# Row sums of four heads in one transfer on ScalarE's queue, decay rows of a pair in one load from DRAM, normalise steps two to a slot, and constants moved off VectorE, in a kernel of forgetting attention followed by a gated feed-forward block

## The chip, the cores and the metric

The kernel runs on one core of a Trainium2 chip. The metric is the device time of one execution, in microseconds (us). Each version was run several times, in alternation with the kernel before on the same chip, and the medians are quoted. The span of a profiled execution is some 2 us shorter than its time; where stages are compared, spans are used.

## The reference

For 8 batches of 8 heads (64 heads in all), 576 positions and a head dimension of 64, causal attention is computed with a decay: `cum` is the running sum of `log(clip(f))`, and `cum[i] - cum[j]` is added to the scaled score of positions i and j. The heads are put side by side and go through a gated feed-forward block (FFN).

```python
scores = scale * np.matmul(q, k.transpose(0, 1, 3, 2))
cum = np.cumsum(np.log(np.clip(f, 0.0001, 1.0)), axis=-1)
scores = scores + cum[:, :, :, None] - cum[:, :, None, :]     # where not causal: -1e9
attn = softmax(scores)                                        # row sums + 1e-9
x = (attn @ v).transpose(0, 2, 1, 3).reshape(4608, 512)
g = x @ w_gate                                                # 512 -> 1536
out = (g * sigmoid(g) * (x @ w_val)) @ w_out                  # 1536 -> 512
```

## The kernel before

The kernel works in slots, a quarter of a head each. A table `todo` says what is issued in which slot; instructions keep that order on each engine. Heads come in pairs, and pairs in groups of four heads. The decay is added by TensorE: q and k get four more rows, so that the scores matmul contracts 68 rows. The value matmul has columns of ones next to v, so it also yields the row sums of exp.

From slot 47 on, the FFN of the first eight heads runs between the attention of the next eight, on the same engines. The parts that the change touches:

```python
    def rows(p):                       # decay rows of a pair: four small transfers
        b = p % NBUF
        hs = slice(2 * p, 2 * p + 2)
        nc.sync.dma_start(out=QT[b][D : D + 1], in_=cq[hs])
        for r in range(3):
            nc.sync.dma_start(out=KT[b][D + 1 + r : D + 2 + r, :, :S], in_=ck[hs, r])

    def collect(h):                    # row sums of one head, spread over 32 partitions
        g, j = h // GH, h % GH
        ...
        nc.sync.dma_start(out=SC[g][j * n : (j + 1) * n, :], in_=E[h][row : row + 1, :])

    def recip(g):                      # one reciprocal for four heads, then to DRAM
        rc = rp.tile([P, GH * S // P], F32, name="rc", tag="rc")
        nc.vector.reciprocal(rc, SC.pop(g))
        nc.sync.dma_start(out=rc_dram[g].rearrange("(p c) -> p c", p=P), in_=rc)

    def spread(g):                     # broadcast of the reciprocals, in two halves
        ...
            nc.sync.dma_start(
                out=rb[a * D : (a + 1) * D],
                in_=src[a].unsqueeze(0).to_broadcast([D, GH // 2, S]),
            )
    ...
        at(s0 - 14, rows, p)
    ...
        at(s0 + 4 + LAG, collect, h)
        if h % GH == GH - 1:
            g = h // GH
            at(s0 + 6 + LAG, recip, g)
            at(s0 + 8 + LAG, spread, g)
            for j in range(GH):
                at(s0 + 12 + LAG + j, normalise, g * GH + j)      # one to a slot
```

`normalise` multiplies a head's values by its reciprocals on VectorE and writes `xT`, which FFN reads. All loads of q, k and v go through SyncE's queue; the FFN weights go through GpSimd's, in ten chunks.

The softmax here doesn't subtract the row's maximum and nothing guards it: scores larger than these inputs give would overflow.

Of the kernel before, what the change touches and what calls it, by code (L numbers as in the profile page):

```python
# [11 lines left out]
ALU = mybir.AluOpType  # L12
# [12 lines left out]
NSLOT = len(BANKS)  # L25
LAG = 3


@with_exitstack
def kernel(ctx, tc, q, k, v, f, w_gate, w_val, w_out, out):  # L30
# [22 lines left out]
    ptp = ctx.enter_context(tc.tile_pool(name="ptp", bufs=3))  # L53
    evp = ctx.enter_context(tc.tile_pool(name="evp", bufs=8))
    rp = ctx.enter_context(tc.tile_pool(name="rp", bufs=2))
    ps_ffn = ctx.enter_context(tc.tile_pool(name="ps_ffn", bufs=4, space=PSUM))
    ps_s = ctx.enter_context(tc.tile_pool(name="ps_s", bufs=2, space=PSUM))
    ps_t = ctx.enter_context(tc.tile_pool(name="ps_t", bufs=1, space=PSUM))
    ps_o = ctx.enter_context(tc.tile_pool(name="ps_o", bufs=1, space=PSUM))
    rc_dram = nc.dram_tensor("rc_d", (BH // GH, GH * S), F32, kind="Internal").ap()  # L60
    order = ctx.enter_context(tc.manual_schedule())

    NBUF = 3
    QT = [consts.tile([KR, 2, S], BF16, name=f"QT{i}") for i in range(NBUF)]
    KT = [consts.tile([KR, 2, NB * P], BF16, name=f"KT{i}") for i in range(NBUF)]
    VB = [consts.tile([P, NB, 2, P], BF16, name=f"VB{i}") for i in range(NBUF)]
    cq = consts.tile([BH, S], BF16, name="cq")
    ck = consts.tile([BH, 3, S], BF16, name="ck")
    wg = wpool.tile([P, KD, DFF], BF16, name="wg")
# [22 lines left out]
    def rows(p):  # L92
        b = p % NBUF
        hs = slice(2 * p, 2 * p + 2)
        nc.sync.dma_start(out=QT[b][D : D + 1], in_=cq[hs])
        for r in range(3):
            nc.sync.dma_start(out=KT[b][D + 1 + r : D + 2 + r, :, :S], in_=ck[hs, r])

    def cast(p, nm):
        if nm == "v":  # L100
            b = p % NBUF
            vn = nat.pop(("v", p))
            for j in range(2):
                nc.gpsimd.tensor_copy(VB[b][:, : NB - 1, j, j * D : j * D + D], vn[:, : NB - 1, j])
                nc.gpsimd.tensor_copy(VB[b][:LAST, NB - 1, j, j * D : j * D + D], vn[:LAST, NB - 1, j])
            return
        t = bfp.tile([P, NB, 2 * D], BF16, name=f"b_{nm}", tag=f"b_{nm}")
        src = nat.pop((nm, p)).rearrange("p n h d -> p n (h d)")
        nc.gpsimd.tensor_copy(t[:, : NB - 1], src[:, : NB - 1])  # L109
        nc.gpsimd.tensor_copy(t[:LAST, NB - 1], src[:LAST, NB - 1])  # L110
        nat["b" + nm, p] = t

    def transposes(p, nm):
        dst = (QT if nm == "q" else KT)[p % NBUF]
        src = nat.pop(("b" + nm, p))
        t = ps_t.tile([P, S], BF16, name="tp", tag="t")
        for n in range(NB):
            w = P if n < NB - 1 else LAST
            nc.tensor.transpose(t[:, n * P : n * P + w], src[:w, n, :], ident[:w, :w])  # L119
        for a in range(2):  # L120
            nc.vector.tensor_copy(dst[:D, a, :S], t[a * D : (a + 1) * D])  # L121

    PT, O, E = {}, {}, {}

    def qk(h, i):
# [6 lines left out]
        for kt, q0, w in BANKS[i]:  # L132
            nc.tensor.matmul(  # L133
                s[:, c : c + w], KT[b][:, j, kt * P : (kt + 1) * P], QT[b][:, j, q0 : q0 + w],
                start=True, stop=True,
            )
            c += w
        off = OFFS[i]
        nc.scalar.activation(pt[:, off : off + c], s[:, :c], AF.Exp, scale=0.125)  # L139
        c = off  # L140
        for kt, q0, w in BANKS[i]:
            if q0 <= kt * P:
                m = min(P, w)
                nc.gpsimd.affine_select(  # L144
                    out=pt[:, c : c + m], in_=pt[:, c : c + m],
                    pattern=[[1, m]], compare_op=ALU.is_ge, fill=0.0, base=0, channel_multiplier=-1,
                )
            c += w

    def pv(h, i):  # L150
# [15 lines left out]
        if last:  # L166
            if half == 0:
                E[h] = evp.tile([P, S], F32, name="ev", tag="ev")
            dst = E[h][:, q_lo : q_lo + q_n]
            if h < H:  # L170
                nc.vector.tensor_copy(dst, o[:, :q_n])
            else:
                nc.scalar.activation(dst, o[:, :q_n], AF.Copy)
            O.pop((h, half))

    SC, RB = {}, {}

    def collect(h):
        g, j = h // GH, h % GH
        if j == 0:  # L180
            SC[g] = rp.tile([P, GH * S // P], F32, name="sc", tag="sc")
        row = D if j % 2 == 0 else 0
        n = P // GH
        nc.sync.dma_start(out=SC[g][j * n : (j + 1) * n, :], in_=E[h][row : row + 1, :])

    def recip(g):
        rc = rp.tile([P, GH * S // P], F32, name="rc", tag="rc")
        nc.vector.reciprocal(rc, SC.pop(g))  # L188
        nc.sync.dma_start(out=rc_dram[g].rearrange("(p c) -> p c", p=P), in_=rc)

    def spread(g):
        rb = rp.tile([P, GH // 2, S], F32, name="rb", tag="rb")
        src = rc_dram[g].rearrange("(r a s) -> a r s", a=2, s=S)
        for a in range(2):
            nc.sync.dma_start(
                out=rb[a * D : (a + 1) * D],
                in_=src[a].unsqueeze(0).to_broadcast([D, GH // 2, S]),
            )
        RB[g] = rb

    def normalise(hd):
        g, j = hd // GH, hd % GH
        a = j % 2
        b0 = (hd // H) * S
        nc.vector.tensor_mul(  # L205
            xT[a * D : (a + 1) * D, (hd % H) // 2, b0 : b0 + S],
            E.pop(hd)[a * D : (a + 1) * D],
            RB[g][a * D : (a + 1) * D, j // 2],
        )
# [38 lines left out]
    with tc.tile_pool(name="ini", bufs=1) as ini:  # L248
        lf = ini.tile([BH, S], F32, name="lf")
        nc.scalar.dma_start(out=lf, in_=f.rearrange("b h s -> (b h) s"))  # L250
        for part in (0, 1, 2):
            load(0, "q", part)
            load(0, "k", part)
        for part in (0, 1, 2):
            load(0, "v", part)
        ident = consts.tile([P, P], BF16, name="ident")
        make_identity(nc, ident[:, :])
        zero = ini.tile([BH, S], F32, name="zero")
        nc.gpsimd.memset(zero, 0.0)
        for i in range(NBUF):  # L260
            nc.vector.memset(QT[i][D:KR], 1.0)
            nc.vector.memset(KT[i][D:KR], 1.0)
            nc.gpsimd.memset(KT[i][:, :, S:], 0.0)
        nc.vector.tensor_scalar(out=lf, in0=lf, scalar1=1e-4, scalar2=1.0, op0=ALU.max, op1=ALU.min)
        nc.scalar.activation(lf, lf, AF.Ln)
        cum = ini.tile([BH, S], F32, name="cum")
        nc.vector.tensor_tensor_scan(out=cum, data0=lf, data1=zero, initial=0.0, op0=ALU.add, op1=ALU.add)
        nc.scalar.activation(cq, cum, AF.Copy, scale=8.0)
        nc.vector.tensor_scalar_mul(ck[:, 0], cum, -8.0)
        r1 = ini.tile([BH, S], F32, name="r1")  # L270
        nc.vector.scalar_tensor_tensor(out=r1, in0=cum, scalar=-8.0, in1=ck[:, 0], op0=ALU.mult, op1=ALU.subtract)
        nc.vector.tensor_copy(ck[:, 1], r1)
        nc.vector.tensor_sub(ck[:, 2], r1, ck[:, 1])
        for i in range(NBUF):
            nc.vector.memset(VB[i], 1.0)
            nc.vector.memset(VB[i][LAST:, NB - 1], 0.0)
    fp = ctx.enter_context(tc.tile_pool(name="fp", bufs=3))
# [9 lines left out]
    for p in range(NP):  # L287
        s0 = 2 * NSLOT * p
        if p > 0:
            n = 0  # L290
            for nm in ("q", "k", "v"):
                for part in range(3):
                    at(s0 - 24 + n, load, p, nm, part)
                    n += 1
        at(s0 - 14, rows, p)
        at(s0 - 11, cast, p, "q")
# [4 lines left out]
    for h in range(BH):  # L301
# [3 lines left out]
        for i in range(NSLOT):  # L305
            at(s0 + i + LAG, pv, h, i)
        at(s0 + 4 + LAG, collect, h)
        if h % GH == GH - 1:
            g = h // GH
            at(s0 + 6 + LAG, recip, g)  # L310
            at(s0 + 8 + LAG, spread, g)
            for j in range(GH):
                at(s0 + 12 + LAG + j, normalise, g * GH + j)

# [6 lines left out]
    for c in range(4):  # L321
        lo, hi = c * DFF // 4, (c + 1) * DFF // 4
        at(NSLOT * (4 + 2 * c), weights, wg, w_gate, lo, hi, True)
        at(NSLOT * (4 + 2 * c) + 2, weights, wv, w_val, lo, hi, True)
    for c in range(2):
        at(NSLOT * (12 + 2 * c), weights, wo, w_out, c * KF // 2, (c + 1) * KF // 2, False)


    ffn = ffn_stream()
    PER_TILE = 2 * KF * KD + KF * MT // P  # L330
    first = NSLOT * (H - 1) + 12 + LAG + GH
    n_mm = 0
    end = NSLOT * BH + LAG + 12 + GH
    for s in range(min(todo), end):
# [40 lines left out]
```

## Time and profile before

| | before |
|---|---|
| time, median of three runs | 486.08 us (485.72 to 486.36) |
| span of the profiled run | 486.3 us |
| TensorE busy | 86% |
| first scores matmul | 21.5 us |
| first gate matmul (FFN begins) | 96.6 us |
| first output matmul of token tile 0 | 132.6 us |
| the same of tile 5 (attention still running) | 366.1 us |

How to read such a profile: the share of a whole span averages over stages that have different limits. The slices show where the stages lie. Within a stage, the waits say which engine stood for what, and the engine's order in time says why the thing it stood for was late. The prediction quotes the lines of this profile.

### The profile page before, as it was taken

How to read it: one execution, taken by the hardware profiler on the slowest of the kernel's cores; microseconds unless marked ns; L12 is line 12 of the kernel's file. 1: busy time of each engine (PE TensorE's matmuls, PEld its weight loads, DVE VectorE, ACT ScalarE, POOL GpSimd, SP SyncE). 2: the span in 40 equal slices, each digit the busy share in tenths (PEclk: the TensorE clock that was granted, in tenths of full speed). 3: DMA queues.
4: the chain of work that ended last, by engine and by line, in shares of the span. 5: the costliest groups of instructions: out<-in, count | busy, mean ns of one | idle time of the engine just before them, and what ended most of it. 6: DMA issues, size and time to landing. Idle time of an engine off the chain costs nothing.

```text
span 486.3 us, 7925 instructions
## 1 busy us (share of the span) xinstructions
PE 420.5 (86%) x2470; PEld 228.3 (47%) x2512; DVE 280.1 (58%) x458; ACT 241.5 (50%) x516; POOL 201.1 (41%) x596
## 2 busy tenths in 40 slices
PE   0295374398899999999999999999899999999996
PEld 0163242254455555555555555555455554444442
DVE  7742250445936784586468556936593676473570
ACT  2253133256456666666666556656565664232321
POOL 3275285145355455455545464545454631000000
PEclk9999999999999999999999999999999999999999
DMA  5358499589364536453746464555455120401102
GB/s 107 74 119 144 106 150 189 112 139 168 84 166 120 124 90 161 125 124 89 171 115 134 107 165 108 127 129 143 109 122 135 55 51 1 137 0 44 44 0 88
DMA packets 136794, 53.18 MB, mean 109 GB/s; under 512 B 122096, under 2 KB 127984, under 8 KB 136752
## 3 DMA queue, kind: packets, MB, share of 16 engines
q1 hardware_dynamic: 130880, 47.80, 41.0%
q0 software_dynamic: 5792, 4.72, 7.1%
q8 instruction: 20, 0.33, 0.3%
q14 instruction: 22, 0.18, 0.1%
q10 hardware_dynamic: 80, 0.15, 0.1%
HBM read 47.33 MB, written 9.58 MB: 117 GB/s over the span
## 4 chain that ended last, share of the span: by engine, by line
PE 70%; DMA 13%; DVE 8%; issue 3%; SPq 2%; ACT 2%; POOL 1%; DVEq 0%; ACTq 0%; POOLq 0%
PE fo L238 18%; PE gp L221 16%; PE vp L229 16%; PE s L133 7%; DMA rb<-rc_d 6%; PE tp L119 4%; DMA sc<-ev 3%; DMA nat_q<-in_q_dram 3%; DVE xT L205 2%; DMA rc_d<-rc 1%; DVE th L225 1%; ACT pt L139 1%; POOL pt L144 1%; SPq L82 1%; DMA nat_k<-in_k_dram 0%
## 5 line engine op out<-in xcount | busy, mean ns | idle before, releaser
L139 ACT ACTIVATE pt<-s 128x384 bf16<-128x384 f32 (+2 forms) x256 | 128.3, 503 | 132.2 <-PE s L133 131.3
L144 POOL TENSOR_SCALAR_AFFINE_SELECT pt<-pt 128x128 bf16<-128x128 bf16 (+1 forms) x320 | 99.6, 322 | 188.3 <-ACT pt L139 187.7
L221 PE MATMUL gp<-xT,wg 128*128 128x512 bf16 x412 | 116.1, 380 | 5.9 <-DVE th L225 4.4
L229 PE MATMUL vp<-xT,wv 128*128 128x512 bf16 x422 | 117.8, 379 | 2.1 <-DVE hh L232 1.5
L238 PE MATMUL fo<-wo,hh 128*128 128x512 bf16 x420 | 102.2, 378 | 0.7
L225 DVE SCALAR_TENSOR_TENSOR th<-th,gp 128x512 f32<-128x512 f32 x108 | 74.2, 687 | 48.8 <-ACT th L224 48.0
L224 ACT ACTIVATE th<-gp 128x512 f32<-128x512 f32 x108 | 64.6, 598 | 42.0 <-PE gp L221 40.2
L232 DVE TENSOR_TENSOR hh<-th,vp 128x512 bf16<-128x512 f32 x108 | 74.2, 687 | 10.0 <-PE vp L229 0.6
L205 DVE TENSOR_TENSOR xT<-ev,rb 64x576 bf16<-64x576 f32 x64 | 52.8, 825 | 40.0 <-DMA rb<-rc_d 38.8
L221 PEld LDWEIGHTS <-wg 128*128 128x128 bf16 x432 | 39.8, 97 | 39.8 <-issue 4.7
L238 PEld LDWEIGHTS <-hh 128*128 128x128 bf16 x432 | 39.5, 97 | 38.9
L229 PEld LDWEIGHTS <-wv 128*128 128x128 bf16 x432 | 39.4, 97 | 38.0 <-issue 3.0
L242 ACT ACTIVATE ot<-fo 128x512 f32<-128x512 f32 x36 | 21.5, 597 | 32.4 <-PE fo L238 29.2
L133 PE MATMUL s<-QT_90,KT_93 68*128 68x320 bf16 (+4 forms) x154 | 32.5, 286 | 1.2 <-DVE KT_93 L121 0.5
L188 DVE RECIPROCAL rc<-sc 128x18 f32<-128x18 f32 x16 | 4.2, 265 | 50.4 <-DMA sc<-ev 43.7
L133 PE MATMUL s<-QT_91,KT_94 68*128 68x320 bf16 (+4 forms) x154 | 32.6, 284 | 0.4
L161 PEld LDWEIGHTS <-VB_98 128*128 128x128 bf16 x140 | 12.5, 103 | 39.7 <-issue 14.7
L133 PE MATMUL s<-QT_92,KT_95 68*128 68x320 bf16 (+4 forms) x140 | 29.8, 286 | 0.4
L119 PE MATMUL tp<-ident,b_k 128*128 128x128 bf16 (+1 forms) x160 | 18.4, 232 | 11.8 <-DVE QT_90 L121 9.8
L119 PE MATMUL tp<-ident,b_q 128*128 128x128 bf16 (+1 forms) x160 | 18.4, 232 | 9.7 <-POOL b_q L109 9.7
L119 PEld LDWEIGHTS <-b_k 128*128 128x128 bf16 (+1 forms) x160 | 13.8, 105 | 22.4 <-issue 13.5
L119 PEld LDWEIGHTS <-b_q 128*128 128x128 bf16 (+1 forms) x160 | 13.7, 105 | 21.5 <-POOL b_q L109 9.7
(312 smaller groups left out, 413.3 us busy)
## 6 DMA issues: line engine op xcount, KB each, us to landing
rb<-rc_d SPq DMA_DIRECT2D x32, 288.0 KB
out_dram<-ot SPq DMA_DIRECT2D x36, 256.0 KB
nat_q<-in_q_dram SPq DMA_DIRECT2D x64, 128.0 KB
nat_k<-in_k_dram SPq DMA_DIRECT2D x64, 128.0 KB
nat_v<-in_v_dram SPq DMA_DIRECT2D x64, 128.0 KB
wg<-in_moe_w_gate_dram POOLq DMA_DIRECT2D x4, 384.0 KB, 6.2
wv<-in_moe_w_val_dram POOLq DMA_DIRECT2D x4, 384.0 KB, 7.9
wo<-in_moe_w_out_dram POOLq DMA_DIRECT2D x2, 768.0 KB, 9.1
```

Source lines behind the costliest of these rows:

```text
L119: nc.tensor.transpose(t[:, n * P : n * P + w], src[:w, n, :], ident[:w, :w])
L133: nc.tensor.matmul(s[:, c : c + w], KT[b][:, j, kt * P : (kt + 1) * P], QT[b][:, j, q0 : q0 + w], start=True, stop=True,)
L139: nc.scalar.activation(pt[:, off : off + c], s[:, :c], AF.Exp, scale=0.125)
L144: nc.gpsimd.affine_select(out=pt[:, c : c + m], in_=pt[:, c : c + m], pattern=[[1, m]], compare_op=ALU.is_ge, fill=0.0, base=0, channel_mu ...
L205: nc.vector.tensor_mul(xT[a * D : (a + 1) * D, (hd % H) // 2, b0 : b0 + S], E.pop(hd)[a * D : (a + 1) * D], RB[g][a * D : (a + 1) * D, j / ...
L221: nc.tensor.matmul(g_, wg[:, ko, fs], xT[:, ko, ts], start=(ko == 0), stop=(ko == KD - 1))
L224: nc.scalar.activation(th, g_, AF.Tanh, scale=0.5)
L225: nc.vector.scalar_tensor_tensor(out=th, in0=th, scalar=1.0, in1=g_, op0=ALU.add, op1=ALU.mult)
L229: nc.tensor.matmul(v_, wv[:, ko, fs], xT[:, ko, ts], start=(ko == 0), stop=(ko == KD - 1))
L232: nc.vector.tensor_mul(h_, th, v_)
L238: nc.tensor.matmul(o, hh[fc][:, ms * P : (ms + 1) * P], wo[:, fc, :], start=(fc == 0), stop=(fc == KF - 1))
L242: nc.scalar.activation(ot, o, AF.Copy, scale=0.5)
```

## The change

The intent is to relieve SyncE, which issues nearly all transfers, and VectorE. Four decay-row transfers of a pair become one load from a copy in DRAM; q and k of a pair share a tile `QK` for this. Four row-sum transfers of a group become one, on ScalarE's queue, where the reciprocal's store and the broadcast go too. The normalise steps move later and come two to a slot. Memsets move from VectorE to GpSimd, k of the first two pairs is loaded through ScalarE's queue, and the weights are issued a little earlier. Some parts are not in the cuts below: the v casts of the first six pairs move to VectorE, evictions write 65 rows instead of 128 and stay on VectorE for four heads more. The core of the diff, with cuts:

```diff
+NORM = 18
...
-    evp = ctx.enter_context(tc.tile_pool(name="evp", bufs=8))
+    evp = ctx.enter_context(tc.tile_pool(name="evp", bufs=2))
...
     def rows(p):
-        nc.sync.dma_start(out=QT[b][D : D + 1], in_=cq[hs])
-        for r in range(3):
-            nc.sync.dma_start(out=KT[b][D + 1 + r : D + 2 + r, :, :S], in_=ck[hs, r])
+        nc.sync.dma_start(
+            out=QK[p % NBUF][D:KR, :, :S],
+            in_=dec_dram[2 * p : 2 * p + 2].rearrange("j w r s -> r (j w) s"),
+        )
...
-        nc.sync.dma_start(out=SC[g][j * n : (j + 1) * n, :], in_=E[h][row : row + 1, :])
+        nc.scalar.dma_start(out=SC[g], in_=E[g][D : D + 1].rearrange("p j s -> p (j s)"))
...
-        nc.sync.dma_start(out=rc_dram[g].rearrange("(p c) -> p c", p=P), in_=rc)
+        nc.scalar.dma_start(out=rc_dram[g].rearrange("(p c) -> p c", p=P), in_=rc)
...
+        nc.scalar.dma_start(
+            out=RB[g].rearrange("p j s -> p (j s)"), in_=rc_dram[g].unsqueeze(0).to_broadcast([D, GH * S])
+        )
...
-            nc.vector.memset(QT[i][D:KR], 1.0)
-            nc.vector.memset(KT[i][D:KR], 1.0)
-            nc.gpsimd.memset(KT[i][:, :, S:], 0.0)
+            nc.gpsimd.memset(QK[i][:, 1::2, S:], 0.0)
+            nc.gpsimd.memset(VB[i][:, :, :, D:], 1.0)
...
+        nc.scalar.dma_start(out=dec_dram, in_=dec)
...
-            at(s0 + 6 + LAG, recip, g)
-            at(s0 + 8 + LAG, spread, g)
+            at(s0 + 4 + LAG, collect, g)
+            at(s0 + 10 + LAG, recip, g)
+            at(s0 + 13 + LAG, spread, g)
             for j in range(GH):
-                at(s0 + 12 + LAG + j, normalise, g * GH + j)
+                at(s0 + NORM + LAG + j // 2, normalise, g * GH + j)
...
-        at(NSLOT * (4 + 2 * c), weights, wg, w_gate, lo, hi, True)
+        at(NSLOT * (3 + 2 * c), weights, wg, w_gate, lo, hi, True)
```

## The prediction

> **What bounds the kernel now.** I read the page first, then its slices, the sums by window, the waits, the SyncE queue in order of time, and single groups. TensorE is busy for 86% of 486.3 us, which alone would say "TensorE-bound, nothing to gain"; the slices say where that is untrue.
>
> ```profile
> PE   0295374398899999999999999999899999999996
> ...
> DMA  5358499589364536453746464555455120401102
> ```
>
> Each digit is a slice of 12.2 us. From slice 10 on TensorE is at 8 or 9 tenths; before it, holes. The windows (us; then busy time and count of PE, PEld, DVE, ACT, POOL; clock; DMA share; GB/s) put numbers on it:
>
> ```profile
> 25.00:36.00 11.00, 10.71 (x60) 7.04 (x59) 5.60 (x13) 6.02 (x12) 8.54 (x30) 1.00 0.53 120
> 36.00:57.00 21.00, 7.24 (x39) 4.46 (x38) 3.99 (x10) 4.01 (x8) 6.99 (x21) 1.00 0.68 119
> 57.00:73.00 16.00, 12.67 (x69) 7.95 (x68) 8.51 (x16) 6.79 (x14) 12.51 (x32) 1.00 0.88 155
> 73.00:97.00 24.00, 9.69 (x47) 5.51 (x47) 5.14 (x11) 6.94 (x17) 9.17 (x29) 1.00 0.85 149
> 97.00:125.00 28.00, 24.45 (x147) 13.10 (x148) 16.24 (x28) 15.01 (x33) 12.63 (x38) 1.00 0.79 142
> 125.00:225.00 100.00, 97.71 (x621) 54.38 (x632) 66.94 (x111) 61.58 (x138) 50.94 (x152) 1.00 0.52 126
> ```
>
> So three stages: a start until the first scores matmul at 21.5 us; attention alone until the first gate matmul at 96.6 us, with TensorE idle for about half of it; then attention and FFN together, 98% busy. Only the first two can yield much. What stops the second is in the waits (engine, line, what it waited for; total us, times, longest) and in SyncE's queue (start, duration):
>
> ```profile
> DVE rc L188 <- DMA sc<-ev: 43.7, 12, 14.0
> ...
> PE o_559 L161 <- DVE ev L171: 13.5, 1, 13.5
> ```
>
> ```profile
> 43.77 0.60 SPq L184 DMA_DIRECT2D sc<-ev  x1
> 44.42 0.57 SPq L82 DMA_DIRECT2D nat_k<-in_k_dram  x1
> 45.05 0.63 SPq L87 DMA_DIRECT2D nat_k<-in_k_dram  x1
> 45.80 1.07 SPq L82 DMA_DIRECT2D nat_v<-in_v_dram  x2
> 46.97 0.55 SPq L184 DMA_DIRECT2D sc<-ev  x1
> 47.95 0.66 SPq L87 DMA_DIRECT2D nat_v<-in_v_dram  x1
> 48.73 1.07 SPq L82 DMA_DIRECT2D nat_q<-in_q_dram  x2
> 49.90 0.67 SPq L95 DMA_DIRECT2D QT_91<-cq  x1
> 50.62 1.79 SPq L97 DMA_DIRECT2D KT_94<-ck  x3
> 52.46 0.68 SPq L87 DMA_DIRECT2D nat_q<-in_q_dram  x1
> 53.23 0.54 SPq L82 DMA_DIRECT2D nat_k<-in_k_dram  x1
> ```
>
> The last fence is one pair of heads: nine loads, four decay rows, two row sums, 15 issues from 43.77 to 53.77, with hardly a gap. SyncE needs **10.0 us a pair, 0.67 us an issue**. TensorE, while undisturbed (25 to 36 us), starts a head every 3.62 us (scores of head 2 at 28.67, head 3 at 32.30), 7.24 us a pair. SyncE therefore falls behind; VectorE stands at the reciprocal, in its order, for a row sum that SyncE has not yet issued; evictions and transposed copies lie behind it, and TensorE behind those. The bound of this stage is SyncE's issue time.
>
> **What the Trainium skill says.** (1) "DMA: Bandwidth & Descriptors", section "Issuing engines are not separate DMA queues": transfers of all queues interleave on the same 16 engines, and another issuer saves only the sequencer's time, "usually small relative to the DMA itself". The trace agrees on what would be saved but not that it is small: at 0.54 to 0.68 us an issue it bounds a stage. (2) "Perfetto Trace Analysis", section "DMA Instruction — HWDGE (DVE, Sync)": a profiled issue starts when its semaphores are satisfied and ends before the data have moved. So 0.6 us is sequencer time; the chain shows landings apart (sc 1.89 us, rc_d 1.64, rb 4.29 for the first group). (3) "TensorE: Matmul & The Clock Gate", Part 1: 1.2 GHz cold, 2.4 GHz after some 3.4 us of sustained activity. Both speeds are in the trace: the longest value matmul (320 columns) takes 474 ns before FFN starts and 310 after. But TensorE is 97% busy for 11 us (25 to 36) and stays slow, so I count attention alone at the cold rate whatever the change does.
>
> **The change part by part.** A slot is a quarter of a head: 0.906 us cold.
>
> *Decay rows and row sums leave SyncE.* Four row transfers of a pair become one load; two row sums, and each group's reciprocal and broadcast, go to ScalarE's queue, one transfer each per four heads. SyncE keeps 10 issues a pair: 10 x 0.67 = 6.7 us, below TensorE's 7.24. It stops being the bound, barely. ScalarE gains 3 x 16 = 48 issues x 0.6 = 29 us over the kernel; it is busy 62% in the mixed stage, so this fits, but its order now contains waits: for the reciprocal, then for its landing in DRAM (1.64 us against three slots, 2.7 us cold). I charge 1.5 us.
>
> *Constants off VectorE.* Before, VectorE's six small memsets (1.02 and 1.12 us) hold the decay arithmetic to 8.6 us, and three VB memsets of 1.14 us hold the first transposed copy to 19.15. After: VectorE does about 2304 columns of memset (2.0 us at 0.885 ns a column, from 1.02 us for 1152). ScalarE first issues seven loads (0.8 to 4.9 us at 0.58), loads its table (1.28) and takes the logarithm (0.68): 6.9. Scan 1.64 and arithmetic 0.45 + 0.75 + 0.45 + 0.75: 11.1. Two copies 0.94, the v cast about 0.7, transposes of k 0.76, first k copy 0.46, partly overlapping: first scores at about **13.6 us instead of 21.5**, 8 us won. Decay rows issued at 11.3 and landing near 13.3 fit.
>
> *Normalise later.* FFN starts at slot 51 instead of 47, the last normalise has the same distance from the end; the chain sums to xT has 15 slots for 8. This costs 4 slots of attention without FFN, but that attention is work done: afterwards one head less remains.
>
> *Attention alone:* 51 x 0.906 = 46.2 us, against 75.1 before for 47 slots (floor 42.6, so 32.5 us of stalls). FFN would start at 13.6 + 46.2 = 59.8. I add two kinds of stall. DMA: windows 57 to 97 show shares of 0.85 to 0.88, and the same weights and loads now come in 46 us instead of 75; with loads 24 slots ahead I charge 3 us. VectorE: four normalises of 0.75 in a row, v casts now on VectorE for six pairs, and a broadcast that may land late (4.3 to 8.7 us in the chain, against five slots = 4.5) for two groups: 4 us. FFN start **67 us**.
>
> *Afterwards.* Before: 486.3 - 96.6 = 389.7 us. In the mixed stage 32 slots take 46.7 us (fo of tile 0 at 134.27, of tile 5 at 367.71, over five), of which 144 FFN matmuls x 0.2165 = 31.2, leaving 1.9 us a head: minus 1.9. From 96.6 to 134.27 the 21.3 slots take 37.7 us instead of 31.1, so 6.6 us are stalls of SyncE's lag; I take back 4. V casts as two wide ones and the two diagonals of a bank in one select lighten GpSimd, which bounds nothing here: 0.
>
> Sum: 67 + 389.7 - 1.9 - 4 + 1.5 = **452.3 us**, 7% less.
>
> **The rivals.** (a) *DMA becomes the bound of the first stage.* For: share 0.88 in 57:73 while only some 4.5 heads ran; per pair it would have to carry loads, two weight chunks and half a broadcast in 7.24 us. Against: most weights are needed late, loads are well ahead. If true, FFN starts at 75 to 80 and the time is 460 to 465. (b) *ScalarE's queue becomes the blocker.* For: exp, tanh and evictions stand behind a transfer that waits for DRAM. Against: three slots are 4.4 us in the mixed stage. If each of 13 later groups costs 1 us, about 464. (c) *evp of two groups.* Group g+2's first eviction (slot 16g+35) comes right after normalise of g (16g+33, 34); a late broadcast stops TensorE at once. Included with 4 us; twice that gives 456. (d) *TensorE turns warm early,* since stalls no longer interrupt it: attention alone could run at nearer 2.6 us a head than 3.6 (estimate: ScalarE 2.0 us a head plus hand-offs), about 440. Against: 11 unbroken us did not do it. (e) *Everything hidden:* the mixed stage is at 98%; if early stalls were compensated later, nothing would change. Against: total TensorE work is fixed, and idle time before 97 us is never caught up.
>
> **Range and chances.** The start's 8 us and some 22 us of SyncE stalls rest on different mechanisms; losing half of either still leaves over 2%. Low end 442: no stalls and a little more recovered later. High end 464: rival a or b. A gain below 2% (over 476.4) needs both a and b in full.
>
> **What would show it.** First scores near 13.6 us (right if 12.5 to 15.5). First gate matmul at 60 to 72. VectorE's wait for row sums, 43.7 us, under 8. SyncE's decay-row issues 128 to 32, no sc or rb on it. Mixed stage at 46 to 47 us per 32 slots; over 48 means ScalarE's queue costs. DMA share over 0.95 with TensorE waiting for loads would mean rival a; value matmuls of 320 columns near 310 ns before FFN, rival d. I am wrong if attention alone stays above 60 us.

## The result and the profile after

| | before | after |
|---|---|---|
| time, median of 4 runs each | 486.22 us (485.72 to 486.81) | 474.56 us (474.04 to 475.7) |
| ratio | | 0.9763 (95% interval 0.9742 to 0.9784) |
| span of the profiled run | 486.3 us | 472.8 us |

The change made the kernel 2.4% faster. The direction was predicted; the size was not: 452.3 us was forecast, the range ended at 464, and about a third of the forecast gain came.

The page of the kernel after, its header, TensorE's total, and the slices (11.8 us each) of TensorE and of the DMA engines:

```profile
span 472.8 us, 7493 instructions
...
PE 428.9 (91%) x2512; PEld 230.4 (49%) x2512; DVE 273.9 (58%) x468; ACT 237.4 (50%) x508; POOL 177.6 (38%) x462
...
PE   0498577799999999999999999999999999999996
...
DMA  7589999962667256726672666166604022201002
```

Counted from 0, TensorE's slices 4 to 7 now read 5, 7, 7, 7, where they read 3, 7, 4, 3 before: the holes of the early stage are shallower. But they lie exactly under slices in which the DMA engines are full: 9, 9, 9, 9. Before, those slices read 4, 9, 9, 5.

The windows of the kernel after (columns as in the prediction: busy time of PE, PEld, DVE, ACT, POOL, granted clock, DMA share, GB/s):

```profile
25.00:50.00 25.00, 21.87 (x117) 13.85 (x116) 12.74 (x31) 12.05 (x26) 15.62 (x39) 1.00 1.00 178
50.00:75.00 25.00, 17.34 (x93) 10.91 (x92) 12.45 (x27) 8.76 (x19) 15.85 (x38) 1.00 1.12 195
75.00:100.00 25.00, 20.15 (x92) 9.60 (x91) 12.00 (x20) 9.57 (x22) 8.38 (x21) 0.86 0.92 172
```

The DMA share reaches 1.12; a share above 1 counts packets that overlap on an engine. The granted clock of 0.86 in the third line belongs to a stretch of slow matmuls that ends near 91 us (below). The clock column is no safe sign of it: in t1, a run below, the matmuls of this stretch are as slow, and its clock reads 1.00.

SyncE's queue in the kernel after, around one decay row load (start, duration; x2 is two issues with the time between them):

```profile
33.93 0.44 SPq L94 DMA_DIRECT2D QK_93<-dec_d  x1
34.47 1.40 SPq L83 DMA_DIRECT2D nat_v<-in_v_dram  x2
36.76 0.84 SPq L88 DMA_DIRECT2D nat_v<-in_v_dram  x1
41.62 0.92 SPq L83 DMA_DIRECT2D nat_q<-in_q_dram  x2
```

One decay issue a pair instead of four, no row sums, and idle time between issues (4 us before 41.62): SyncE no longer limits the stage by issuing. VectorE's wait for row sums, 43.7 us before, is gone from the waits altogether. What stands there in its place is waits of ScalarE (engine, line, waited for; total us, times, longest):

```profile
ACT pt L139 <- DMA nat_k<-in_k_dram: 9.2, 1, 9.2
...
ACT pt L139 <- DMA QK_93<-dec_d: 4.2, 1, 4.2
...
ACT pt L139 <- DMA rc_d<-rc: 3.7, 1, 3.7
```

Line 139 is the exp of the scores, which reads neither `nat_k` nor `rc_d`. The order in time around the 9.2 us explains it:

```profile
75.22 0.61 SPq L88 DMA_DIRECT2D nat_k<-in_k_dram  x1
...
84.64 0.50 ACTq L184 DMA_DIRECT2D sc<-ev  x1
85.19 0.44 ACT L139 ACTIVATE pt<-s 128x320 bf16<-128x320 f32 x1 [9.23 <-DMA nat_k<-in_k_dram]
...
85.94 0.75 PE L119 MATMUL tp<-ident,b_k 128*128 128x128 bf16 x5 [3.77 <-ACT ev L176]
```

ScalarE stood at its issue of `sc` until a load that SyncE had issued at 75.22 had landed, 9.3 us later; exp, tanh and the evictions stood behind it, and TensorE lost 3.8 us. In the built program (this was read there, not in a trace), the transfers that SyncE and ScalarE issue share eight completion semaphores in turn, and each one waits for the transfer eight before it. Between 75.22 and 84.64 SyncE issued exactly seven. So a queue of its own did not free ScalarE from SyncE's loads.

The stop goes with a second cost, which the experiments below were not made for. Four `vp` matmuls of FFN before the stop, and four later:

```profile
79.86 1.91 PE L223 MATMUL vp<-xT,wv 128*128 128x512 bf16 x4
...
98.04 1.02 PE L223 MATMUL vp<-xT,wv 128*128 128x512 bf16 x4
```

TensorE runs at its slow rate through attention alone, and in the changed kernel it stays slow in FFN too: the gate matmul takes 584 to 634 ns until 90.9 us, 14.8 us after FFN's start, and 378 later. In the kernel before the slow ones end 2.1 us after FFN's start (96.6 to 98.7), in e5 below 5.0 us after (78.2 to 83.2). From the first gate matmul to tile 0, TensorE is idle for 5.1 us and busy for 36.3 in the changed kernel, 1.3 and 32.6 in e5. So 3.7 of the 7.6 us between them are longer matmuls and not waiting; between t1 and e5 it is 2.6 of 6.5.

Finally, two normalises to a slot. First VectorE, then TensorE, twice each, in the kernel after:

```profile
53.40 3.42 DVE L201 TENSOR_TENSOR xT<-ev,rb 64x576 bf16<-64x576 f32 x4
...
177.88 3.13 DVE L201 TENSOR_TENSOR xT<-ev,rb 64x576 bf16<-64x576 f32 x4
```

```profile
57.39 0.59 PE L163 MATMUL o_678<-pt,VB_97 128*128 128x320 bf16 x2 [2.60 <-DVE ev L174]
...
181.07 0.38 PE L215 MATMUL gp<-xT,wg 128*128 128x512 bf16 x1 [0.37 <-DVE xT L201]
```

Four normalises now run without anything between them. While they do, an eviction (57.39) or the gate matmul (181.07) waits. In the mixed stage each such wait is small, but it comes with every group: 32 slots take 46.92 us each time.

Prediction and result by stage (spans, us; the predicted marks are those of the prediction's sum, with the first output matmul of a tile as the mark):

| stage | before | predicted | after | after less predicted |
|---|---|---|---|---|
| to the first scores | 21.5 | 13.6 | 18.9 | +5.3 |
| attention alone, to the first gate matmul | 75.1 | 53.4 | 57.2 | +3.8 |
| on to the first output matmul of tile 0 | 36.0 | 32.0 | 41.4 | +9.4 |
| on to that of tile 5 | 233.4 | 233.4 | 234.6 | +1.2 |
| rest | 120.2 | 119.9 | 120.7 | +0.8 |
| span | 486.3 | 452.3 | 472.8 | +20.5 |

### The profile page after: what moved, and what is told of

The parts are those of the page before. It is cut to its first block, busy times and chain, and to the rows that moved or that the text cites. A ratio compares the mean times of both kernels' runs of the same rounds, so it can differ in the third digit from the quotient of the medians.

```text
span 472.8 us, 7493 instructions
## 1 busy us (share of the span) xinstructions
PE 428.9 (91%) x2512; PEld 230.4 (49%) x2512; DVE 273.9 (58%) x468; ACT 237.4 (50%) x508; POOL 177.6 (38%) x462
## 3 DMA queue, kind: packets, MB, share of 16 engines
q10 hardware_dynamic: 8460, 11.07, 10.9%
## 4 chain that ended last, share of the span: by engine, by line
PE 68%; DVE 16%; DMA 8%; ACT 3%; issue 2%; POOL 1%; ACTq 0%; SPq 0%; DVEq 0%; POOLq 0%
PE gp L215 16%; PE vp L223 16%; PE fo L232 15%; DVE xT L201 9%; PE s L133 8%; PE tp L119 5%; DMA nat_k<-in_k_dram 3%; DVE th L219 2%; DMA rb<-rc_d 2%; DMA rc_d<-rc 2%; DVE hh L226 1%; ACT pt L139 1%; DMA QK_93<-dec 1%; ACT th L218 1%; DVE QK_93 L121 1%
## 5 line engine op out<-in xcount | busy, mean ns | idle before, releaser
L139 ACT ACTIVATE pt<-s 128x384 bf16<-128x384 f32 (+2 forms) x256 | 127.7, 501 | 135.5 <-PE s L133 83.2
L148 POOL TENSOR_SCALAR_AFFINE_SELECT pt<-pt 128x128 bf16<-128x128 bf16 (+2 forms) x256 | 89.8, 352 | 203.6 <-ACT pt L139 196.9
L215 PE MATMUL gp<-xT,wg 128*128 128x512 bf16 x432 | 123.2, 384 | 7.3 <-DVE xT L201 3.9
L223 PE MATMUL vp<-xT,wv 128*128 128x512 bf16 x432 | 121.4, 383 | 0.0
L232 PE MATMUL fo<-wo,hh 128*128 128x512 bf16 x432 | 104.5, 378 | 0.0
L226 DVE TENSOR_TENSOR hh<-th,vp 128x512 bf16<-128x512 f32 x108 | 74.2, 687 | 11.6 <-PE vp L223 1.0
L201 DVE TENSOR_TENSOR xT<-ev,rb 64x576 bf16<-64x576 f32 x64 | 49.4, 771 | 7.9 <-DMA rb<-rc_d 7.1
L133 PE MATMUL s<-QK_93 68*128 68x320 bf16 (+4 forms) x154 | 33.8, 295 | 6.7 <-DMA QK_93<-dec 3.4
L236 ACT ACTIVATE ot<-fo 128x512 f32<-128x512 f32 x36 | 21.5, 597 | 29.9 <-PE fo L232 26.7
L121 DVE COPY QK_94<-tp 64x576 bf16<-64x576 bf16 x44 | 19.9, 453 | 27.1 <-PE tp L119 26.1
L121 DVE COPY QK_93<-tp 64x576 bf16<-64x576 bf16 x44 | 19.9, 453 | 23.5 <-PE tp L119 22.5
L133 PE MATMUL s<-QK_95 68*128 68x320 bf16 (+4 forms) x140 | 29.9, 286 | 3.4 <-ACT pt L139 3.2
L133 PE MATMUL s<-QK_94 68*128 68x320 bf16 (+4 forms) x154 | 32.6, 284 | 0.4
L121 DVE COPY QK_95<-tp 64x576 bf16<-64x576 bf16 x40 | 18.1, 453 | 23.7 <-PE tp L119 22.8
L119 PEld LDWEIGHTS <-b_k 128*128 128x128 bf16 (+1 forms) x160 | 14.0, 106 | 25.7 <-issue 17.8
L119 PE MATMUL tp<-ident,b_q 128*128 128x128 bf16 (+1 forms) x160 | 18.8, 235 | 6.3 <-POOL b_q L109 6.3
```

The source lines that it names most:

```text
L119: nc.tensor.transpose(t[:, n * P : n * P + w], src[:w, n, :], ident[:w, :w])
L121: nc.vector.tensor_copy(QK[p % NBUF][:D, 2 * a + w_, :S], t[a * D : (a + 1) * D])
L133: nc.tensor.matmul(s[:, c : c + w], QK[b][:, 2 * j + 1, kt * P : (kt + 1) * P], QK[b][:, 2 * j, q0 : q0 + w], start=True, stop=True,)
L139: nc.scalar.activation(pt[:, off : off + c], s[:, :c], AF.Exp, scale=0.125)
L148: nc.gpsimd.affine_select(out=diag, in_=diag, pattern=pat, compare_op=ALU.is_ge, fill=0.0, base=0, channel_multiplier=-1,)
L201: nc.vector.tensor_mul(xT[a * D : (a + 1) * D, (h % H) // 2, b0 : b0 + S], E[g][:D, j], RB[g][:, j])
```

## The experiments

Theories at the outset: **D**, the DMA engines are full in the first stage and transfers land late; **Q**, the change put transfers in ScalarE's order, and what they wait for stops it; **N**, two normalises to a slot hold VectorE; **S**, the start is later than counted. All runs have the state fast unless said; every time is a median of four. The runs came in four batches, each on another chip and beside the kernel before (485.29 to 487.09 us), so the ratios are the safer comparison between batches. "Gate" and "tile 0" are the first gate matmul and the first output matmul of tile 0 in the profiled run, "pace" is the time of 32 slots in the mixed stage (us). Of the kernel after these are 76.1, 117.5 and 46.92.

| run | us | ratio to before (95%) | gate | tile 0 | pace |
|---|---|---|---|---|---|
| e1_sums_on_sync | 477.91 | 0.9838 (0.9787 to 0.9890) | 78.0 | 120.4 | 46.92 |
| e2_late_weights | 469.91 | 0.9681 (0.9611 to 0.9751) | 68.5 | 111.1 | 46.92 |
| e3_no_weights (wrong) | 463.91 | 0.9557 (0.9498 to 0.9616) | 71.4 | 106.5 | 46.91 |
| p_rows_alone | 466.94 | 0.9606 (0.9555 to 0.9658) | 84.8 | 116.3 | 45.84 |
| e5_normalise_spaced | 463.64 | 0.9528 (0.9473 to 0.9582) | 78.2 | 112.1 | 45.84 |
| e6_early_table | 472.25 | 0.9706 (0.9634 to 0.9778) | 74.5 | 115.7 | 46.92 |
| c1_all_three | 463.62 | 0.9529 (0.9474 to 0.9584) | 73.9 | 112.9 | 45.84 |
| c2_rows_spread_weights (profile slow) | 462.53 | 0.9498 (0.9432 to 0.9564) | 82.2 | 117.5 | 45.84 |
| s1_spaced_no_weights (wrong) | 458.44 | 0.9416 (0.9354 to 0.9479) | 74.4 | 108.6 | 45.84 |
| s2_before_no_weights (wrong) | 478.54 | 0.9833 (0.9777 to 0.9889) | 87.5 | 121.5 | 46.5 to 47.5 |
| s3_spaced_late | 459.98 | 0.9449 (0.9384 to 0.9513) | 69.9 | 106.2 | 45.84 to 46.92 |
| s4_rows_late | 461.85 | 0.9488 (0.9430 to 0.9545) | 75.2 | 111.3 | 45.85 |
| t1_third_buffer | 473.71 | 0.9748 (0.9702 to 0.9794) | 76.1 | 116.5 | 46.92 |
| t2_spaced_two_buffers | 466.08 | 0.9589 (0.9562 to 0.9615) | 82.2 | 114.3 | 45.84 to 46.52 |
| t3_spaced_early_late | 463.88 | 0.9549 (0.9511 to 0.9587) | 75.0 | 109.2 | 45.85 to 46.97 |

### Is it ScalarE's queue? (e1_sums_on_sync)

```diff
-        nc.scalar.dma_start(out=SC[g], ...)          # likewise rc_dram[g] and RB[g]
+        nc.sync.dma_start(out=SC[g], ...)
```

> The changed kernel with the three transfers of a group's row sums (sums, reciprocals, broadcast) issued from SyncE instead of ScalarE; nothing else. Theory Q (ScalarE's in-order stream stops: it stood 3.1 us before 47.85 and 3.6 us before 69.21 until the reciprocals had landed in DRAM, and 5.5 us before 84.64 until a load of SyncE had landed): these stops vanish, TensorE's idle stretches of 1.9, 2.5 and 3.8 us with them, and the time falls by about 8 us to 466. Theory D (DMA saturation alone, wherever the transfers are issued): VectorE waits at the reciprocal and at the normalise instead, the time stays within 2 us of 474.6.

It was not faster than the change but 3 us slower. The stops moved to VectorE, as TensorE's order in this run shows:

```profile
63.07 0.58 PE L163 MATMUL o<-pt,VB 128*128 128x320 bf16 x2 [8.29 <-DVE ev L174]
...
85.80 0.58 PE L215 MATMUL gp<-xT,wg 128*128 128x512 bf16 x1 [7.20 <-DVE xT L201]
```

Whoever issues the group's transfers, someone stands for them. Q as the cause falls: it only says which engine is stopped. The queue move itself is worth keeping.

### Is it the DMA engines? (e2_late_weights, e3_no_weights)

e2 issues all weight chunks but the first about ten slots ahead of their use (the "5 slots" of its expectation is a slip). e3 loads only the first chunk of each weight and sets the rest to 0, so that its result is wrong.

```diff
-        at(NSLOT * (3 + 2 * c), weights, wg, ...)
-        at(NSLOT * (3 + 2 * c) + 2, weights, wv, ...)
+        at((28, 45, 51, 57)[c], weights, wg, ...)      # e2
+        at((32, 47, 53, 59)[c], weights, wv, ...)
-        at(NSLOT * (11 + c), weights, wo, ...)
+        at((63, 67)[c], weights, wo, ...)
```

```diff
     def weights(t, src, lo, hi, cols):
-        if cols:
+        if lo > 0:
+            nc.gpsimd.memset(t[:, :, lo:hi] if cols else t[:, lo:hi], 0.0)   # e3
+        elif cols:
```

> The changed kernel with the weight loads set later, each chunk some 5 slots before its first use: gate chunks at slots 28, 45, 51, 57 instead of 12, 20, 28, 36, value chunks at 32, 47, 53, 59 instead of 14, 22, 30, 38, output chunks at 63, 67 instead of 44, 48. Theory D: the DMA share in 25 to 75 us falls from 1.0 to 1.1 to about 0.75, reciprocals land in 2 us instead of 5, the first gate matmul comes at 68 to 71 instead of 76.1, and the time falls by 6 to 10 us. Theory Q alone: landings on ScalarE's path stay as long as the queue has loads, and the time stays within 3 us of 474.6.

> Wrong result on purpose: of each weight only the first chunk is loaded, the others are set to zero by GpSimd at the same slots, so the same matmuls run without most of the weights' DMA traffic. It bounds theory D from above. D: first gate matmul at 66 to 69, time 458 to 464. Q alone: within 3 us of 474.6, since ScalarE still waits for landings in DRAM and for SyncE's loads.

Without the weights' traffic the changed kernel takes 463.91 us, 10.7 less; with the traffic moved, FFN starts at 68.5 instead of 76.1, but 4.7 us are all that is kept (its profile also started 3.3 us earlier, see e6). The same stop comes later: ScalarE issues a `sc` at 101.95 after 7 us. TensorE in e2:

```profile
103.25 0.75 PE L119 MATMUL tp<-ident,b_k 128*128 128x128 bf16 x5 [4.63 <-ACT ev L176]
```

In e2, too, TensorE is slower after the stop: the gate matmul took 376 to 378 ns just before it and takes up to 634 from 105.1 to 108.2 us. That suggests the stop as the reason; no run was made to show it. D holds as a cost of some 10 us: e3 starts like the change (18.3 and 18.9), so the start has no part in it. A caution on e3, s1 and s2: their memsets add work to GpSimd (18.8 us busy in 25 to 50 us of s1 against 15.6 in the changed kernel), so what they save may be too small.

### The decay rows alone (p_rows_alone)

The kernel before with one part of the change: the decay rows go to DRAM once, and a pair's come in one load. The edit also takes the six memsets of `QT` and `KT` off VectorE (two of `dec` come instead), spreads pair 0's rows over two queues and issues the others four slots later (cut below).

```diff
-        nc.sync.dma_start(out=QT[b][D : D + 1], in_=cq[hs])
-        for r in range(3):
-            nc.sync.dma_start(out=KT[b][D + 1 + r : D + 2 + r, :, :S], in_=ck[hs, r])
+        nc.sync.dma_start(
+            out=QK[p % NBUF][D:KR, :, :S],
+            in_=dec_dram[2 * p : 2 * p + 2].rearrange("j w r s -> r (j w) s"),
+        )
```

> The kernel before with one part of the change: the decay rows of a pair in one load from DRAM (and the tiles merged for it). Row sums stay on SyncE head by head, the VB constants stay on VectorE. If SyncE's issues bound the first stage (15 issues of 0.67 us a pair, now 12), the pair period falls from 10.0 to about 8.0 us and the first gate matmul comes 6 to 9 us earlier than 96.6: 477 to 480 us. If DMA traffic was the bound already before, within 2 us of 486.2.

One part alone takes the time to 466.94 us, lower than the whole change and far below both expectations. By stage, the 20.4 us of span that it gains are 3.7 at the start (first scores at 17.8), 8.1 in attention alone, 4.5 on to tile 0 and 4.2 in the five rounds after it. Fewer issues can therefore account for at most 8.1 us in the stage that they were said to bound. So the rest of the change costs more than it gives: 474.56 - 466.94 = 7.6 us (different chips; the ratios, 0.9763 and 0.9606, say the same). Its mixed stage runs at 45.84 us per 32 slots, and it still has one normalise to a slot. That pointed to N. (The kernel before has one to a slot as well and takes 46.7; there VectorE waits 12.4 us for row sums between 133 and 366 us, and in this run not at all.) The waits of VectorE in its first stage:

```profile
DVE xT L202 <- DMA rb<-rc_d: 15.6, 4, 10.3
...
DVE rc L185 <- DMA sc<-ev: 11.5, 2, 8.1
```

The wait for row sums has shrunk with the issues on SyncE, though all the row sums are still on its queue: in the same stage of the kernel before it was 26.8 us in two waits.

### One normalise to a slot, and which of its two edits does it (e5, t1, t2)

e5 puts the four normalises in four slots, the last a slot later than before, and gives the evicted heads a third buffer. t1 has the buffer alone. t2 has the spacing alone, with the first normalise two slots earlier.

```diff
-    evp = ctx.enter_context(tc.tile_pool(name="evp", bufs=2))
+    evp = ctx.enter_context(tc.tile_pool(name="evp", bufs=3))                    # e5, t1
-                at(s0 + NORM + LAG + j // 2, normalise, g * GH + j)
+                at(s0 + NORM - 1 + LAG + j, normalise, g * GH + j)               # e5
+                at(s0 + NORM - 2 + LAG + j, normalise, g * GH + j)               # t2
```

> The changed kernel with the four normalises of a group one to a slot (as before) instead of two to a slot, starting one slot earlier and ending one later; the eviction tile gets a third buffer for it. Theory N (pairs of normalises hold VectorE 1.5 us, tanh product and gate matmul behind them: TensorE stops 0.38 us twice in every 32 slots of the mixed stage, 46.92 us where the one-part kernel has 45.84): 45.8 us per 32 slots, 6 to 8 us less in all, 467 to 469. Rival (the 46.92 come from ScalarE's queue or from the 65-row evictions): 46.9 per 32 slots and 473 to 475.

> The changed kernel with a third buffer for the evicted heads of a group, its normalises in pairs as they were. The run with spaced normalises had both edits. Theory S (the spacing did it): no gain, 473 to 476 us, 46.9 us per 32 slots. Rival B (two buffers: the first eviction of a group waits for the normalises of the group before last): most of the 10.9 us, 464 to 467, and 45.84 us per 32 slots.

> The changed kernel with one normalise to a slot, but two buffers as in the change: the first comes two slots earlier, the last stays where it was. Theory S: 463 to 466 us, 45.84 us per 32 slots. Rival B: 472 to 476. If the broadcast, which now has three slots instead of five before the first normalise, is late: 467 to 471 with VectorE waiting for rb in each group, and over 46.5 us per 32 slots.

e5 gains 10.9 us on the change, more than expected, t1 less than 1 (473.71), t2 8.5 (466.08). So it is the spacing. The cleanest pair is t1 and e5, which differ in nothing else and both have first scores at 15.6: 10.1 us. The buffer, rival c of the prediction, is not a cause by itself. In spans e5 is 11.6 us shorter than the change (472.8 to 461.2): 5.4 until tile 0 (4.4 against t1; the change started 3.3 us later), then 5.4 in the five rounds of the mixed stage (5 x 1.08), the rest after. Around the start of FFN, TensorE in e5 has only these waits left:

```profile
77.52 0.50 PE L163 MATMUL o<-pt,VB 128*128 128x256 bf16 x2 [1.94 <-DVE QK L121]
...
80.38 0.59 PE L215 MATMUL gp<-xT,wg 128*128 128x512 bf16 x1 [1.09 <-DVE xT L201]
```

From the first gate matmul to tile 0 it takes 33.8 us against 41.4. The 9.2 us for which ScalarE stood are absent in e5 and t2, and there in t1 (9.2) and e6 (9.7). Without pairs the stops on a load are shorter, none over 6.2 us (c1). Why the spacing shortens them was not traced.

### Is it the start? (e6_early_table)

In the changed kernel, ScalarE loads its table only after its k loads, two of which are held:

```profile
3.94 2.11 ACTq L83 DMA_DIRECT2D nat_k<-in_k_dram  x2
6.85 0.67 ACTq L88 DMA_DIRECT2D nat_k<-in_k_dram  x1
7.55 1.28 ACT L264 ACT_TABLE_LOAD   x1 [7.55 <-DMA nat_k<-in_k_dram]
```

```profile
18.88 0.48 PE L133 MATMUL s<-QK_93 68*128 68x256 bf16 x2 [3.37 <-DMA QK_93<-dec]
```

e6 makes ScalarE load the table at 0.8 us, by a logarithm of a constant, and puts pair 1's k loads on SyncE.

```diff
+        pre = ini.tile([1, 1], F32, name="pre")
+        nc.vector.memset(pre, 1.0)
+        nc.scalar.activation(pre, pre, AF.Ln)
...
-                load(p, "k", part, nc.scalar)
+                load(p, "k", part, nc.scalar if p == 0 else nc.sync)
```

> The changed kernel with ScalarE's table for the logarithm loaded first (by a one-element logarithm) and the k loads of pair 1 issued from SyncE, so the logarithm no longer stands behind loads that wait for other loads. First scores at 14 to 15.5 us instead of 18.9. If the first stage is a chain of waits, the time falls by 3 to 5 us (470 to 471); if DMA traffic bounds that stage, the start is absorbed and the time stays within 2 us of 474.6.

The first scores come at 15.9 us, the time falls by 2.3, which the intervals of the two ratios do not tell from nothing. And this is not a clean proof of S: e1, e5 and t1, whose start is that of the change, had the first scores at 15.6, t2 at 18.5. The same start falls in one of two ways, and one wait tells them apart: in the late way TensorE waits 3.3 to 3.4 us for the decay rows (the change, e3, t2, t3: 18.3 to 18.9), in the early way it does not (e1, e2, e5, s1, s3, t1: 15.4 to 15.8). e6 waits 3.3 us as well, so like against like its first scores are some 3 us earlier. What decides between the ways was not found. The four executions of one run may hold both: the spans of s3 are 456.2, 456.3, 459.8 and 459.8.

### Do the causes add? (c1, c2, s1, s2, s3, s4, t3)

c1 has e5's and e6's edits and weights spread evenly over slots 12 to 64. c2 has p_rows_alone with its weights spread over slots 12 to 60. s1 has e5's and e3's edits, s3 e5's and e2's; s2 is the kernel before with e3's edit; s4 is p_rows_alone with its weights about ten slots ahead of use. t3 has t2's spacing, the third buffer and e2's weights. They contain no other edits; for example the weights of c1 and c2:

```diff
+        at((12, 26, 40, 54)[c], weights, wg, ...)      # c1; wv (19, 33, 47, 59), wo (50, 64)
+        at((12, 24, 37, 50)[c], weights, wg, ...)      # c2; wv (18, 30, 43, 55), wo (46, 60)
```

> The changed kernel with the spaced normalises, the early table and the weight chunks spread evenly over slots 12 to 64. If the three terms (mixed stage 6 to 8, start 0 to 4, weights' contention 4 to 6) are separate, they add up: 457 to 463 us. If DMA contention in the first stage eats whatever the others free, 465 to 468.

c1 is no better than e5 (463.62 against 463.64): spreading evenly and the early table bring nothing on top of spacing. A miss for the view that the three add.

> The one-part kernel (decay rows in one load, 466.9) with its weight chunks spread over slots 12 to 60. Its first stage ends with the first gate matmul at 84.8, 24 us above its undisturbed pace. If weights' traffic stretches that stage, 460 to 463; if SyncE's 12 issues a pair still do, within 2 us of 466.9.

c2 is at 462.53, 4.4 us below p_rows_alone; its profiled run was slow, so only its fast times count.

> The changed kernel with one normalise to a slot and with only the first chunk of each weight loaded (the rest set to 0, so a wrong result on purpose). Apart, the first was worth 10.9 us against the changed kernel (474.6 to 463.6) and the second 10.7 (463.9). Theory M (two separate causes: transfers of the first stage land late because the DMA engines are full, and normalises come in pairs): they add, 452 to 455 us, first gate matmul at 66 to 71. Rival O (both remove the same stalls: the late broadcast and the pair of normalises behind it): they do not add, 460 to 464 us.

s1 came out between the two expectations: 458.44, 16.1 us below the change, where the two edits apart give 10.9 and 10.7, together 21.6. They overlap by 5.5 us. This fits the stop at 84.64, which either edit removes (s1 and e3 have none over 4.8 us).

> Control: the kernel before with the same weights left out (wrong result on purpose). Theory M' (a new wait: the kernel before was bound by SyncE's issues in that stage and not by the DMA engines, so their traffic became a cost only with the change): within 1% of before, 481 to 486 us. Rival W (the weights' traffic cost as much already before, so it took nothing of the expected gain): 10 us less, 474 to 477 us, a ratio near 0.98.

The control refuted what I had come to believe, that the change had created the DMA cost. The kernel before gains 8.5 us without the weights, nearly as much as the changed kernel. It is visible in one place. The issue of the last `sc` and VectorE's reciprocal in the kernel before:

```profile
79.69 0.88 SPq L184 DMA_DIRECT2D sc<-ev  x1
```

```profile
86.25 0.27 DVE L188 RECIPROCAL rc<-sc 128x18 f32<-128x18 f32 x1 [12.76 <-DMA sc<-ev]
```

and in s2:

```profile
74.88 0.60 SPq L184 DMA_DIRECT2D sc<-ev  x1
```

```profile
77.09 0.27 DVE L188 RECIPROCAL rc<-sc 128x18 f32<-128x18 f32 x1 [3.17 <-DMA sc<-ev]
```

Issue and landing together made this wait 9.6 us shorter, which is all of the 9.1 us by which FFN starts earlier. From the issue's start to the reciprocal it takes 2.2 us in s2 and 6.6 before, so 4.4 of it is landing; the rest is the issue itself, 4.8 us earlier.

> A version that could beat both: one normalise to a slot, and the later weight chunks issued about ten slots ahead of their first use (result correct). Apart they gave 10.9 and 4.7 us. If they add: 459 us (457 to 461). If the fuller stage after the start of FFN takes it back, as in the run with late weights alone (a stall of 4.6 us at 103): 463 to 465, no better than spacing alone.

> The kernel before with the decay rows of a pair in one load, and the weight chunks issued about ten slots ahead of first use. With the rows alone it was 466.9, with the chunks spread evenly 462.5. If that stage is now bound by late landings: 460 to 463. If SyncE's issues (12 a pair, 8.0 us against TensorE's 7.24) bound it still: 466 to 467, and the first scores at 17.7 as before.

> Spaced normalises that end where the pairs ended, a third buffer, and the later weight chunks ten slots ahead of use: a candidate for the fastest. Against the 459.98 of spacing one slot later with the same weights: the same within 1 us if a slot more or less of distance does not matter, 457 if the FFN start a slot earlier is won, 462 if the broadcast comes late to the first normalise.

s3, with a correct result, takes 459.98 us (458.12 to 461.75). It is faster than before by 5.5% and than the change by 3%. s4 reaches 461.85 with little more than the decay rows, and c2 462.53. The intervals of the three overlap, so the order among them is open. t3 suggests that the spacing should end one slot later: at 463.88 it is slower than s3, and VectorE waits 11.3 us for broadcasts in the first stage, against 7.0 in s3. But its profile fell in the late start (18.4), that of s3 in the early one, and the intervals just touch, so this is not shown. In s3 TensorE's largest waits after 61 us are about 1 us, among them

```profile
101.10 0.52 PE L119 MATMUL tp<-ident,b_k 128*128 128x128 bf16 x5 [1.30 <-ACT ev L176]
...
109.40 0.38 PE L232 MATMUL fo<-wo,hh 128*128 128x512 bf16 x1 [0.92 <-DMA wo<-in_moe_w_out_dram]
```

Its five stages (to the first scores, attention alone, to tile 0, to tile 5, rest) are 15.4, 54.5, 36.3, 230.3 and 119.7 us, 456.2 in sum (one of its two faster executions); predicted were 13.6, 53.4, 32.0, 233.4 and 119.9. With spacing and late weights, the first two stages come within 2 us of the forecast.

## Why the prediction was wrong, and where it was right

By the table, 9.4 of the 20.5 us missed came between the start of FFN and tile 0, 5.3 at the start, and only 3.8 in attention alone, the stage that the prediction worked out most closely.

- **SyncE's issues bound the first stage: right, but not alone.** With three issues less a pair, p_rows_alone gained 8.1 us in attention alone, and SyncE has idle time after the change. A step that failed is "(floor 42.6, so 32.5 us of stalls)" followed by putting all of them to SyncE's issue time: s2 shows that some 9 us of this stage depended on the weights' traffic already before. Those did not go with the issues. A slip besides: "from slice 10 on" should be slice 8, counted from 0; the stage marks do not use it.
- **"With loads 24 slots ahead I charge 3 us": mis-sized.** Rival a was the right mechanism. The DMA share over attention alone went from 0.73 to 1.02, with 1.12 from 50 to 75 us. Small transfers that I took at 1.64 us (`rc_d`) landed in 5.0 us in the first stage (issued at 42.79, ScalarE released at 47.85). The chain of the kernel before already had the sign: the `sc` issued at 79.69 took 6.37 us, and I used the 1.89 of the first group. Without the weights the changed kernel is 10.7 us faster. FFN started at 76.1, inside the 75 to 80 of rival a; its time of 460 to 465 was still too low, as the stage after lost more. I had counted the bytes as fitting, but not what a full DMA stage does to the small transfers on the chain.
- **Rival b, ScalarE's queue: real as a stop, not as a cost of its own.** e1 took the transfers off this queue and lost 3 us. What I missed is that in this program the two queues share their completion semaphores.
- **Normalises: the term "four normalises of 0.75 in a row ... 4 us" was mis-sized, and put in one stage only.** Pairs cost 10.1 us (t1 against e5), 8.5 with two buffers (t2): 4.4 before tile 0 and over 1 us in every 32 slots after. For the mixed stage I charged nothing, and its 46.92 us passed my test of "46 to 47" with this cost in it.
- **First scores at 13.6: wrong by 5.3 us in the profiled run, some 2 in others.** I put the table load at 4.9 us; it started at 7.55, behind loads of ScalarE that were held, and the decay rows landed later than the 2 us I gave them. With the early table they came some 3 us earlier, like against like (e6); what that is worth in time is not clear of the noise.
- **"I take back 4" after the start of FFN: failed.** This was the largest step that failed: the stage took 41.4 us instead of 32.0. The working was off from the start: the first output matmul of tile 0 is at 132.62 and not 134.27, so before there were 4.9 us of stalls to take back and not 6.6. In their place came ScalarE's stop (3.8 us of TensorE's time) and slow matmuls for 14.8 us after FFN's start, which no term foresaw. Even s1 and e5, where the big stops are gone, take 34.
- **Rival c, two eviction buffers: no cost by itself** (t1). **Rival d, a warm TensorE: did not come**; attention alone kept the cold speed, and FFN's first 14.8 us too. **Rival e, everything hidden: did not come**; 2.4% is clear of the noise. **Constants off VectorE** were never run alone; p_rows_alone, which moves six of the memsets among other things, has its first scores 3.7 us earlier.

The two main causes together, pairs and the weights' traffic, make 16.1 of the 22.3 us between 474.56 and 452.3 (s1). In spans s1 lies 4.4 us above the forecast: start +2.2, attention alone +5.3, to tile 0 +2.1, to tile 5 -4.2, rest -1.0. The minus is another mis-sized term: I took the mixed stage of before as it was, and 45.84 us per 32 slots were to be had. Where the 5.3 us come from was not settled; in s3, which does not have the memsets of s1, it is 1.1.

## What to carry to other kernels

When transfers on one queue bound a stage, ask how much of each wait is issue and how much is landing: the time from an issue to its consumer, set against that of a quiet stage, tells them apart, and only the first part goes away with fewer issues. A stage that is shortened by a quarter carries the same bytes in less time, so move traffic that isn't needed there, such as late weights, before counting on its small transfers. Work that is handed out by slots should be spread evenly: two vector instructions of 0.8 us in one slot of 0.9 to 1.5 us cost some 10 us here, about half of what the decay rows' part gave. And look at the durations of matmuls after a stop, not only at the wait: here a stop of 3.8 us went with some 3 us more in slower matmuls.

## What the Trainium skill lacked or had wrong

- "DMA: Bandwidth & Descriptors", section "Issuing engines are not separate DMA queues", calls the issuing time that a second engine saves "usually small relative to the DMA itself". Here 15 issues of 0.67 us a pair filled SyncE for 10.0 us where TensorE needs 7.24, and with three issues less a pair the stage was 8.1 us shorter (p_rows_alone, which has other edits too).
- No page that I read tells what it costs when the program lets transfers of SyncE and ScalarE share completion semaphores in turn: ScalarE stood 9.2 us at an issue because a load of SyncE's, eight transfers earlier, had not landed.
- "DMA: Bandwidth & Descriptors", section "Latency and other measured facts", gives HBM access latency as 0.2 us on average and 2 us at high load. It does not tell how small transfers fare in a stage with full DMA engines: here `rc_d` took about 5 us from issue to release at a DMA share of 1.00, and in the kernel before `sc` took 6.6 us with the weights' traffic and 2.2 without.
- "TensorE: Matmul & The Clock Gate", Part 1, has TensorE warm after some 3.4 us of sustained activity. In all versions attention alone stayed at the cold speed (474 ns for 320 columns against 310 later), though TensorE was 97% busy for 11 us in the kernel before. No run here shows what it lacked. The profile's clock column reads 1.00 for these stretches; only the durations show the state.
